# Key projections alternated on the array's row halves, and the sums over tokens with the values stationary

## The chip, the cores and the metric

The kernel runs on one core of one Trainium2 chip. A core has five engines that run side by side, each with its own queue in program order: TensorE (PE, matrix products; its weight loads are shown as PEld), VectorE (DVE), ScalarE (ACT), GpSimd (POOL) and SyncE (SP, which here issues the DMAs). TensorE reads from SBUF and writes into eight PSUM banks of 512 f32 columns on 128 partitions; GpSimd works on SBUF alone. The metric is the time of one execution on the device in microseconds.

## The reference

There are three stages: attention with a feature map (4 batches, 8 heads, 576 tokens, head size 64, 128 features, so 2 x 128 after the two exponentials), a dense layer pair with `h - tanh(h)` (512 to 2048 to 512), and a weighted mixture of four experts. The change lies in the key side of the first stage:

```python
def phi(x):
    proj = np.einsum('bhsd,df->bhsf', x, w_phi)
    proj = proj - np.max(np.abs(proj), axis=-1, keepdims=True)
    return np.concatenate([np.exp(proj), np.exp(-proj)], axis=-1)
q_p, k_p = (phi(q), phi(k))
kv = np.einsum('bhsf,bhsd->bhfd', k_p, v)      # 256 x 64 per head
z = np.sum(k_p, axis=2)                         # 256 per head
num = np.einsum('bhsf,bhfd->bhsd', q_p, kv)
den = np.einsum('bhsf,bhf->bhs', q_p, z)[..., None] + 1e-06
```

## The kernel before

The 2304 tokens are worked on in eight blocks of 288. Each block first goes through attention and then through the first half of the dense layers (eight of sixteen chunks of 128 hidden features); a second pass does the other eight chunks, and the experts come last. Attention is cut into tasks for two heads at a time: a key task (`k_task`, 16 of them) turns 576 tokens of keys and values of two heads into the sums `kv` and `z`, and a query task (`q_task`, 32 of them) uses them for 288 tokens. The key and query tasks of later blocks are laid between the dense work of earlier ones.

The order of the work is not written out by hand. Every step is a node with an engine, an estimated duration, a due time, the nodes it waits for, and the buffers and PSUM banks that it takes (`add`, `Ring`, `Bank`). `Issue.run` goes through time with these estimates and gives each engine, when it is free, the ready node that is due first; a node that wants a PSUM bank is passed over while none is free. What comes out is a fixed order of instructions on each engine, and on the chip each engine keeps to it. Four of the eight PSUM banks are handed out in this way, the other four accumulate the dense layer's output.

A key task before the change: the keys are loaded with one token of each group of four per column block and transposed (L406, L409) so that head 0 lies on partitions 0 to 63 and head 1 on 64 to 127. `proj` (L417) is called once for each head: four products of 64 x 128 stationary keys with `w_phi` moving (L422), then on VectorE the largest magnitude of each row (L429) and the subtraction (L430), and on ScalarE the two exponentials (L431, L432). The 64 remaining tokens of both heads go through L443 and L447 to L450. Then `mmk` (L455) sums over tokens, in four groups, one for each head and sign: the features are stationary (128 tokens by 128 features) and `vones` moves, which is a block of values beside a block of ones, so that columns 0 to 63 of the result are `kv` and the next ones `z`. Each group has four products (L458) and one for the remaining tokens (L459). ScalarE copies the four results out of one bank (L462) into `kv`, 128 columns for each group, of which the query task reads the first 66 (L532). All these products are in plain f32, and the profile shows each of them as two passes over the array, each with its own weight load; the dense layers use f32r, which is one pass.

On the query side, `proj` (L490) runs products for both heads in turn, head 0 on rows 0 to 63 and head 1 on rows 64 to 127, into two banks. `xf` (L542) and most of the `gl` subtractions (L236) run on GpSimd, and so does the second half of each weight split (L309). VectorE turns the first eight chunks of weights from 64-bit into 32-bit numbers (L300 to L303) during the first blocks.

Of the kernel before, what the change touches and what calls it, by code (L numbers as in the profile page):

```python
# [9 lines left out]
F32 = mybir.dt.float32  # L10
# [61 lines left out]
class Issue:  # L72
# [106 lines left out]
def attention_moe_moe_kernel(  # L179
# [45 lines left out]
    def ring(pool, n, shape, dt, name):  # L225
        return Ring([pool.tile(shape, dt, name=f"{name}{i}") for i in range(n)])
# [11 lines left out]
    def at(bk):  # L238
        return banks[bk.index]
# [12 lines left out]
    wph = const.tile([128, 128], F32R, name="wph")  # L252
    wpl = const.tile([128, 128], F32R, name="wpl")
    b_m = const.tile([128, 1], F32, name="b_m")
    pr = const.tile([128, NTT, E], F32, name="pr")
    prs = const.tile([128, NTT], F32, name="prs")
    vtiles = [att.tile([128, 14 * 64], F32, name=f"vbuf{i}") for i in range(2)]
# [4 lines left out]
    DVE.memset(b_m, THETA2)  # L262
    for vb in vtiles:
        DVE.memset(vb[:, 0:64], 1.0)
        DVE.memset(vb[:, 576:640], 1.0)
        DVE.memset(vb[:, 640:896], 0.0)
        DVE.memset(vb[0:64, 704:768], 1.0)
        DVE.memset(vb[64:128, 832:896], 1.0)
# [90 lines left out]
    kd_r = ring(att, 1, [128, 4, 128], F32, "kd")  # L359
# [3 lines left out]
    kpr_r = ring(att, 1, [128, 2, 128], F32, "kpr")  # L363
    kv_r = ring(att, 6, [128, 2, 2, 128], F32, "kv")
# [17 lines left out]
    kv_of, xt_of = {}, {}  # L382
    n_att = [0, 0]

    def vones(vb, i):
        return vb.rearrange("p (n d) -> p n d", d=64)[:, i:10:9 - i, :]

    def k_task(b, p, t0):
        rb, rrb, vb = kraw.take(), krawr.take(), v_ring.take()
        h = 2 * p  # L390
# [3 lines left out]
        ], due=t0 - 8, bufs=[rb, rrb])  # L394
        vv = vb.t
        ldv = dma([
            (vv[:, 64:576].rearrange("p (h x) -> p h x", h=2), v[b, h:h + 2, 0:512, :].rearrange("h (p r) d -> p h (r d)", r=4)),
            (vv[0:64, 640:704], v[b, h, 512:S, :]),
            (vv[64:128, 768:832], v[b, h + 1, 512:S, :]),
        ], due=t0 - 4, bufs=[vb])  # L400
        kT, km = kT_r.take(), km_r.take()
        ba, bb = Bank(), Bank()
# [11 lines left out]
        a2 = add("DVE", c_dve(64), lambda: DVE.tensor_copy(out=kT.t[:, 512:S], in_=at(bb)[:, 0:64]), [a], t0 + 0.6, [kT], frees=[bb])  # L414
        kps, es = [], []

        def proj(e, due):  # L417
            bk, kd, kp = Bank(), kd_r.take(), kp_r.take()

            def mm():  # L420
                for j in range(4):
                    PE.matmul(  # L422
                        at(bk)[:, j * 128:(j + 1) * 128], lhsT=kT.t[64 * e:64 * e + 64, j * 128:(j + 1) * 128],
                        rhs=wphi[64 * e:64 * e + 64, :], start=True, stop=True,
                    )

            m = km.t[:, 4 * e:4 * e + 4]
            a = add("PE", 0.82, mm, [a1], due, [kT, kd], bank=bk)
            a = add("DVE", c_dve(512), lambda: DVE.tensor_reduce(out=m, in_=at(bk).rearrange("p (j f) -> p j f", f=128), axis=AX.X, op=ALU.max, apply_absolute_value=True), [a], due + 1, [km], frees=[bk])  # L429
            a = add("DVE", c_dve(512), lambda: DVE.tensor_tensor(out=kd.t, in0=at(bk).rearrange("p (j f) -> p j f", f=128), in1=m.unsqueeze(2).to_broadcast([128, 4, 128]), op=ALU.subtract), [a], due + 1, [km, kd], frees=[bk])  # L430
            x1 = add("ACT", c_act(512), lambda: ACT.activation(out=kp.t[:, :, 0, :], in_=kd.t, func=ACTF.Exp), [a], due + 2, [kd, kp])  # L431
            x2 = add("ACT", c_act(512), lambda: ACT.activation(out=kp.t[:, :, 1, :], in_=kd.t, func=ACTF.Exp, scale=-1.0), [a], due + 2, [kd, kp])  # L432
# [15 lines left out]
        a = add("DVE", c_dve(128), lambda: DVE.tensor_scalar(out=kdr.t, in0=at(bk)[:, 0:128], scalar1=km.t[:, 8:9], scalar2=None, op0=ALU.subtract), [a], due + 1, [km, kdr], frees=[bk])  # L448
        r1 = add("ACT", c_act(128), lambda: ACT.activation(out=kpr.t[:, 0, :], in_=kdr.t, func=ACTF.Exp), [a], due + 2, [kdr, kpr])
        r2 = add("ACT", c_act(128), lambda: ACT.activation(out=kpr.t[:, 1, :], in_=kdr.t, func=ACTF.Exp, scale=-1.0), [a], due + 2, [kdr, kpr])  # L450
        bk2, kv = Bank(), kv_r.take()
        last = None
        for e in range(2):
            for ab in range(2):
                def mmk(e=e, ab=ab):  # L455
                    o = at(bk2)[:, (2 * e + ab) * 128:(2 * e + ab + 1) * 128]
                    for j in range(4):
                        PE.matmul(o, lhsT=kps[e].t[:, j, ab, :], rhs=vones(vv, 1 + 4 * e + j), start=j == 0, stop=False)  # L458
                    PE.matmul(o, lhsT=kpr.t[:, ab, :], rhs=vv[:, 640 + 128 * e:768 + 128 * e], start=False, stop=True)  # L459

                last = add("PE", 1.03, mmk, [es[e][ab], (r1, r2)[ab], ldv, last], t0 + 5 + e, [kps[e], kpr, vb, kv], bank=bk2)
        a = add("ACT", c_act(512, True), lambda: ACT.activation(out=kv.t.rearrange("p a b f -> p (a b f)"), in_=at(bk2), func=ACTF.Copy), [last], t0 + 8, [kv], frees=[bk2])  # L462
        kv_of[b, p] = (kv, a)

    def q_task(b, s, p, t0):
        j = 2 * b + s
# [58 lines left out]
        def side(ab):  # L525
            return at(nb[ab])[0:QP, 0:6 * DV].rearrange("p (e r d) -> p e r d", e=2, r=3)

        def mm():
            for ab, x in enumerate((ea, eb)):
                for e in range(2):  # L530
                    for r in range(3):
                        PE.matmul(side(ab)[:, e, r], lhsT=x.t[:, e, r * QP:(r + 1) * QP], rhs=kv.t[:, e, ab, 0:DV], start=True, stop=True)  # L532

        u, dn, xf = u_r.take(), dn_r.take(), xf_r.take()
        a = add("PE", 2.05, mm, [*xe, s2, kvdone], t0 + 5, [ea, eb, kv, u], banks=nb)
# [292 lines left out]
```

## Time and profile before

| what | time |
|---|---|
| median of three runs | 1500.53 us (1497.84 to 1501.63) |
| the profiled execution, as timed | 1499.14 us |
| its span in the profile | 1497.1 us |
| TensorE busy | 1481.9 us, 99% of the span |
| VectorE busy | 704.5 us, 47% |
| ScalarE busy | 521.6 us, 35% |
| GpSimd busy | 277.9 us, 19% |

The page's span is the time from the first to the last instruction of the profiled execution; some 2 us lie around it. A busy share is a mean over the whole kernel, so it hides that the attention stage loads VectorE far more than the later stages do: of the 704.5 us of VectorE, 328 lie in the first 435 us. Products overlap on TensorE, so the duration of one of them is longer than its distance to the next start; prices are read from the distances between starts.

### The profile page before, as it was taken

Reading aid. Unit: us, or ns where it says so; the run is one execution under the profiler, and the core shown is the slowest. Engines: PE = TensorE matmul, PEld = TensorE weight load, DVE = VectorE, ACT = ScalarE, POOL = GpSimd, SP = SyncE. Lnnn points to the kernel's source line nnn. Section 1 sums busy time; section 2 is a strip of 40 time slices with the busy share of each in tenths; the row PEclk is TensorE's granted clock in tenths of the full one; section 3 lists DMA queues with packets and bytes.
Section 4 is the critical chain, followed back from the end, with each engine's and each line's share of the span. In section 5 each row is a group of like instructions: output and inputs, shape, how many; then the busy total and the mean of one; then the engine's idle time right before and its main releaser. Section 6 shows DMA issues by size and latency. Waiting matters only on the chain.

```text
span 1497.1 us, 22821 instructions
## 1 busy us (share of the span) xinstructions
PE 1481.9 (99%) x9120; PEld 1313.8 (88%) x9120; DVE 704.5 (47%) x1440; ACT 521.6 (35%) x1250; POOL 277.9 (19%) x278
## 2 busy tenths in 40 slices
PE   8999999999999999999999999999999999999998
PEld 7889999999999999999888888888888888888887
DVE  6899976656676766665222122222221322222212
ACT  5565654555555655554111111111111111111101
POOL 1233111101013643436010101010101010101000
PEclk8899999999999999999999999999999999999999
DMA  6445642211113421212010000000000000000001
GB/s 173 132 153 184 202 133 64 76 37 57 60 43 109 158 81 64 67 46 80 22 29 15 29 14 29 14 22 22 28 15 28 15 29 15 22 21 7 28 29 70
DMA packets 93753, 90.70 MB, mean 61 GB/s; under 512 B 46160, under 2 KB 74960, under 8 KB 93648
## 3 DMA queue, kind: packets, MB, share of 16 engines
q1 hardware_dynamic: 93488, 89.19, 19.1%
q8 instruction: 72, 1.18, 0.3%
q14 instruction: 33, 0.27, 0.1%
q10 hardware_dynamic: 160, 0.07, 0.0%
HBM read 66.16 MB, written 23.07 MB: 60 GB/s over the span
## 4 chain that ended last, share of the span: by engine, by line
PE 93%; DVE 5%; ACT 1%; issue 0%; DMA 0%; POOL 0%; ACTq 0%; DVEq 0%
PE bank L351 40%; PE acc L351 39%; PE bank L532 4%; PE bank L458 3%; PE bank L422 2%; PE bank L516 1%; PE bank L490 1%; PE bank L459 1%; DVE wtmp L302 1%; DVE hs L585 1%; PE bank L547 0%; PE bank L476 0%; PE bank L406 0%; DVE th L587 0%; DVE wtmp L303 0%
## 5 line engine op out<-in xcount | busy, mean ns | idle before, releaser
L351 PE MATMUL bank<-x2h,wslot 128*128 128x512 f32 (+1 forms) x1280 | 392.0, 371 | 0.0
L776 DVE SCALAR_TENSOR_TENSOR hl<-bank,hh 128x512 fp32r<-128x512 f32 (+1 forms) x160 | 102.2, 639 | 595.5 <-ACT hh L775 595.5
L351 PE MATMUL acc<-wslot,hh 128*128 128x512 f32 x1152 | 356.8, 391 | 0.0
L775 ACT ACTIVATE hh<-bank 128x512 fp32r<-128x512 f32 (+1 forms) x160 | 88.8, 555 | 673.8 <-PE bank L351 673.8
L351 PEld LDWEIGHTS bank<-x2h,wslot 128*128 128x128 f32 x1280 | 233.2, 188 | 47.5
L351 PEld LDWEIGHTS acc<-wslot,hh 128*128 128x128 f32 x1152 | 213.8, 188 | 46.2
L351 PE MATMUL acc<-gh,wslot 128*128 128x288 f32 x1024 | 240.6, 303 | 0.0
L351 PE MATMUL bank<-x2l,wslot 128*128 128x512 f32 (+1 forms) x640 | 237.7, 371 | 0.0
L351 PE MATMUL acc<-wslot,hl 128*128 128x512 f32 x576 | 224.1, 389 | 0.0
L757 POOL TENSOR_TENSOR wslot<-raw,wslot 128x512 fp32r<-128x512 f32 x56 | 71.3, 1297 | 601.4 <-ACT wslot L756 581.8
L351 PEld LDWEIGHTS acc<-gh,wslot 128*128 128x128 f32 x1024 | 173.9, 188 | 3.9 <-issue 3.7
L236 POOL TENSOR_TENSOR gl<-th,gh 128x288 fp32r<-128x288 f32 x112 | 96.8, 865 | 339.2 <-ACT gh L588 225.7
L351 PE MATMUL acc<-gl,wslot 128*128 128x288 f32 x512 | 150.8, 295 | 0.0
L351 PEld LDWEIGHTS bank<-x2l,wslot 128*128 128x128 f32 x640 | 119.9, 187 | 24.0
L351 PEld LDWEIGHTS acc<-wslot,hl 128*128 128x128 f32 x576 | 108.2, 188 | 23.2
L351 PE MATMUL bank<-xt0h,wslot 128*128 128x288 f32 x512 | 115.9, 301 | 2.8 <-ACT wslot L308 1.5
L351 PE MATMUL bank<-xt1h,wslot 128*128 128x288 f32 x512 | 114.4, 298 | 0.0
L587 DVE COPY_PREDICATED th<-sq,hs 128x288 f32<-128x288 int32 x128 | 82.5, 645 | 63.4 <-ACT sq L586 63.3
L351 PEld LDWEIGHTS acc<-gl,wslot 128*128 128x128 f32 x512 | 96.5, 189 | 0.0
L586 ACT ACTIVATE sq<-sq,b_m 128x288 f32<-128x288 f32 x128 | 68.6, 536 | 62.8 <-DVE hs L585 61.8
L351 PEld LDWEIGHTS bank<-xt0h,wslot 128*128 128x128 f32 x512 | 86.4, 190 | 4.6 <-POOL wslot L309 1.8
L794 DVE SCALAR_TENSOR_TENSOR acc<-acc,pr,acc 128x512 f32<-128x512 f32 x126 | 85.9, 743 | 1.2 <-PE acc L351 1.2
(104 smaller groups left out, 1969.6 us busy)
## 6 DMA issues: line engine op xcount, KB each, us to landing
raw<-in_moe_w_dram SPq DMA_DIRECT2D x64, 256.0 KB, 2.9
raw<-in_moe_w_in_dram SPq DMA_DIRECT2D x16, 512.0 KB, 4.0
raw<-in_moe_w_out_dram SPq DMA_DIRECT2D x16, 512.0 KB, 4.4
qraw<-in_q_dram SPq DMA_DIRECT2D x32, 144.0 KB, 2.8
x2s<-x2p SPq DMA_DIRECT2D x8, 576.0 KB, 2.8
x2p<-x2s SPq DMA_DIRECT2D x8, 576.0 KB, 3.8
out_dram<-acc SPq DMA_DIRECT2D x18, 256.0 KB, 2.1
kraw<-in_k_dram SPq DMA_DIRECT2D x16, 256.0 KB, 3.5
```

The costliest lines, as they stand in the source:

```text
L236: return add("POOL", c_pool(n), lambda: POOL.tensor_tensor(out=o, in0=a, in1=b, op=op), deps, due, bufs)
L302: a = add("DVE", c_dve(DM), lambda: DVE.scalar_tensor_tensor(out=t, in0=hi, scalar=0xC0000000, in1=t, op0=ALU.bitwise_and, op1=ALU.bitwise ...
L351: PE.matmul(ps, lhsT=a, rhs=b, start=start and n == 1, stop=stop and n == 3 * len(pairs))
L422: PE.matmul(at(bk)[:, j * 128:(j + 1) * 128], lhsT=kT.t[64 * e:64 * e + 64, j * 128:(j + 1) * 128], rhs=wphi[64 * e:64 * e + 64, :], start ...
L458: PE.matmul(o, lhsT=kps[e].t[:, j, ab, :], rhs=vones(vv, 1 + 4 * e + j), start=j == 0, stop=False)
L532: PE.matmul(side(ab)[:, e, r], lhsT=x.t[:, e, r * QP:(r + 1) * QP], rhs=kv.t[:, e, ab, 0:DV], start=True, stop=True)
L586: x3 = add("ACT", c_act(N, ptr=True), lambda: ACT.activation(out=sq.t, in_=sq.t, func=ACTF.Relu, scale=-1.0, bias=b_m[:, 0:1]), [y3], due ...
L587: y4 = add("DVE", c_dve(N), lambda: DVE.copy_predicated(out=th.t, mask=sq.t.bitcast(I32), data=hs.t), [x3, y2, y3], due + 1.4, [th, sq, hs])
L757: POOL.tensor_tensor(out=wl, in0=src, in1=f32(wh), op=ALU.subtract)
L775: ACT.activation(out=hh[:, 0:n], in_=ps[:, 0:n], func=ACTF.Relu)
L776: DVE.scalar_tensor_tensor(out=hl[:, 0:n], in0=ps[:, 0:n], scalar=0.0, in1=f32(hh[:, 0:n]), op0=ALU.max, op1=ALU.subtract)
L794: DVE.scalar_tensor_tensor(out=acc[:, tt, :], in0=y, scalar=pe, in1=acc[:, tt, :], op0=ALU.mult, op1=ALU.add)
```

## The change

In a key task the two projections become one step: the eight products of both heads alternate, head 0 on rows 0 to 63 of the array and head 1 on rows 64 to 127, into two PSUM banks (the buffer `kd` is doubled for that). In the sums over tokens the roles of the operands are exchanged: a block of values (128 tokens by 64 columns) is stationary and all 256 features of a token block move, so that the result is the transpose of `kv`, head 0 on partitions 0 to 63 and head 1 on 64 to 127 of one bank. The products of the two heads alternate. The sum `z` is made apart: GpSimd adds the four token blocks of each head and the remaining tokens (`pairs`, a second addition, `rest`), and a product with a stationary block of ones sums that over the partitions (`mmz`). ScalarE copies the bank out (`kvT`), TensorE transposes it back in four pieces (`back`), and ScalarE copies `kv` and the column of `z` into a buffer of 66 columns for each group. The blocks of ones between the values go away, and the value buffers shrink.

```diff
-        def proj(e, due):
-            bk, kd, kp = Bank(), kd_r.take(), kp_r.take()
-
-            def mm():
-                for j in range(4):
-                    PE.matmul(
-                        at(bk)[:, j * 128:(j + 1) * 128], lhsT=kT.t[64 * e:64 * e + 64, j * 128:(j + 1) * 128],
-                        rhs=wphi[64 * e:64 * e + 64, :], start=True, stop=True,
-                    )
-
+        pb = [Bank(), Bank()]
+        kds = [kd_r.take(), kd_r.take()]
+
+        def proj():
+            for j in range(4):
+                for e in range(2):
+                    h0 = 64 * e
+                    PE.matmul(at(pb[e])[:, j * 128:(j + 1) * 128], lhsT=kT.t[h0:h0 + 64, j * 128:(j + 1) * 128], rhs=wphi[h0:h0 + 64, :], start=True, stop=True)
+
+        pd = add("PE", 1.05, proj, [a1], t0 + 1.2, [kT, *kds], banks=pb)
...
-        bk2, kv = Bank(), kv_r.take()
-        last = None
+        kss, zs = [], []
         for e in range(2):
-            for ab in range(2):
-                def mmk(e=e, ab=ab):
-                    o = at(bk2)[:, (2 * e + ab) * 128:(2 * e + ab + 1) * 128]
-                    for j in range(4):
-                        PE.matmul(o, lhsT=kps[e].t[:, j, ab, :], rhs=vones(vv, 1 + 4 * e + j), start=j == 0, stop=False)
-                    PE.matmul(o, lhsT=kpr.t[:, ab, :], rhs=vv[:, 640 + 128 * e:768 + 128 * e], start=False, stop=True)
-
-                last = add("PE", 1.03, mmk, [es[e][ab], (r1, r2)[ab], ldv, last], t0 + 5 + e, [kps[e], kpr, vb, kv], bank=bk2)
-        a = add("ACT", c_act(512, True), lambda: ACT.activation(out=kv.t.rearrange("p a b f -> p (a b f)"), in_=at(bk2), func=ACTF.Copy), [last], t0 + 8, [kv], frees=[bk2])
-        kv_of[b, p] = (kv, a)
+            kp, tz, ks = kps[e], tz_r.take(), ks_r.take()
+            h0 = 64 * e
+
+            def pairs(kp=kp, tz=tz):
+                POOL.tensor_tensor(out=tz.t.rearrange("p j f -> p (j f)"), in0=kp.t[:, 0:2].rearrange("p j a f -> p (j a f)"), in1=kp.t[:, 2:4].rearrange("p j a f -> p (j a f)"), op=ALU.add)
+
+            def rest(ks=ks, h0=h0):
+                POOL.tensor_tensor(out=ks.t[h0:h0 + 64], in0=ks.t[h0:h0 + 64], in1=kpr.t[h0:h0 + 64].rearrange("p a f -> p (a f)"), op=ALU.add)
+
+            a = add("POOL", c_pool(512), pairs, es[e], t0 + 4 + e, [kp, tz])
+            a = add("POOL", c_pool(256), lambda tz=tz, ks=ks: POOL.tensor_tensor(out=ks.t, in0=tz.t[:, 0], in1=tz.t[:, 1], op=ALU.add), [a], t0 + 5 + e, [tz, ks])
+            zs.append(add("POOL", c_pool(256), rest, [a, r1, r2], t0 + 5 + e, [ks, kpr]))
+            kss.append(ks)
+        bk2, bk3, kvT, kv = Bank(), Bank(), kvT_r.take(), kv_r.take()
+
+        def mmk():
+            for j in range(5):
+                for e in range(2):
+                    w = vv[:, 512 + 64 * e:576 + 64 * e] if j == 4 else vv[:, 256 * e + 64 * j:256 * e + 64 * j + 64]
+                    x = kpr.t if j == 4 else kps[e].t[:, j]
+                    PE.matmul(at(bk2)[64 * e:64 * e + 64, 0:256], lhsT=w, rhs=x.rearrange("p a f -> p (a f)"), start=j == 0, stop=j == 4)
+
+        def mmz():
+            for e in range(2):
+                PE.matmul(at(bk2)[64 * e:64 * e + 64, 256:512], lhsT=ones, rhs=kss[e].t, start=True, stop=True)
+
+        def back():
+            for i in range(4):
+                PE.transpose(out=at(bk3)[:, i * 128:(i + 1) * 128], in_=kvT.t[:, i * 128:(i + 1) * 128], identity=ident)
...
+        a = add("PE", 2.3, mmk, [*es[0], *es[1], r1, r2, ldv], t0 + 5, [*kps, kpr, vb, kvT], bank=bk2)
+        a = add("PE", 0.46, mmz, [a, *zs], t0 + 7, kss, bank=bk2)
+        a = add("ACT", c_act(512, True), lambda: ACT.activation(out=kvT.t, in_=at(bk2), func=ACTF.Copy), [a], t0 + 8, [kvT], frees=[bk2])
+        a = add("PE", 0.44, back, [a], t0 + 9, [kvT, kv], bank=bk3)
+        a1 = add("ACT", c_act(256, True), lambda: ACT.activation(out=kv_out(0, 64), in_=kv_in(0, 64), func=ACTF.Copy), [a], t0 + 9.5, [kv], frees=[bk3])
+        a2 = add("ACT", 0.1, lambda: ACT.activation(out=kv_out(64, 2), in_=kv_in(1, 2), func=ACTF.Copy), [a], t0 + 9.5, [kv], frees=[bk3])
+        kv_of[b, p] = (kv, [a1, a2])
```

## Rows read from the trace of the kernel before

**Rows 1.** Windows by block: engine busy us (instructions), granted clock, DMA share, GB/s.
```profile
161.40:219.00 57.60, 57.60 (x491) 54.64 (x490) 50.58 (x120) 34.81 (x93) 10.56 (x12) 1.00 0.56 178
219.00:277.10 58.10, 58.10 (x492) 54.96 (x492) 35.58 (x86) 31.09 (x85) 9.65 (x12) 1.00 0.21 62
...
393.30:435.00 41.70, 41.70 (x364) 40.28 (x365) 29.87 (x76) 23.08 (x69) 7.29 (x9) 1.00 0.14 51
```

**Rows 2.** Windows before 161.4 us; order PE, PEld, DVE, ACT, POOL.
```profile
20.00:100.00 80.00, 75.01 (x621) 68.71 (x620) 73.09 (x156) 50.04 (x120) 23.89 (x21) 0.94 0.48 142
100.00:161.40 61.40, 60.55 (x513) 56.71 (x513) 58.09 (x133) 37.83 (x100) 17.34 (x16) 1.00 0.56 170
```

**Rows 3.** Chain of waits from 0 to 161.4 us, shares by line.
```profile
by line: PE bank L458 12.6%; PE bank L532 10.1%; PE bank L351 9.4%; PE bank L422 9.4%; PE acc L351 6.7%; DVE wtmp L302 6.2%; issue 3.6%; PE bank L516 3.1%; DVE wtmp L303 2.9%; PE bank L459 2.9%; DVE km L429 2.3%; DVE wtmp L300 2.3%; DVE kd 
```

**Rows 4.** TensorE in order of time: start us, us, instruction, count.
```profile
101.35 0.40 PE L490 MATMUL bank<-qh,wph 64*128 64x288 f32 x2
101.59 0.30 PE L490 MATMUL bank<-ql,wph 64*128 64x288 f32 x2
101.73 0.30 PE L490 MATMUL bank<-qh,wpl 64*128 64x288 f32 x2
101.95 0.40 PE L351 MATMUL bank<-xt0h,wslot 128*128 128x288 f32 x1
102.19 0.29 PE L351 MATMUL bank<-xt0l,wslot 128*128 128x288 f32 x1
```

**Rows 5.** TensorE in order of time, 241.7 to 246.1 us.
```profile
241.75 0.29 PE L351 MATMUL acc<-gl,wslot 128*128 128x288 f32 x1
241.89 0.29 PE L351 MATMUL acc<-gh,wslot 128*128 128x288 f32 x1
242.11 1.16 PE L422 MATMUL bank<-wphi,kT 64*128 64x128 f32 x8
243.20 1.16 PE L458 MATMUL bank<-vbuf,kp 128*128 128x128 f32 x8
...
244.82 1.05 PE L458 MATMUL bank<-vbuf,kp 128*128 128x128 f32 x8
...
246.06 0.30 PE L351 MATMUL acc<-gl,wslot 128*128 128x288 f32 x1
```

**Rows 6.** Pass durations: L422 min/median/max ns; a group's busy us, mean ns; chain of waits.
```profile
L422 PE MATMUL bank<-wphi,kT x256: 272/272/579, 7.0 to 381.0; 64*128 64x128 f32 x128
...
L351 PE MATMUL bank<-x2h,wslot 128*128 128x256 f32 x256 | 50.4, 281 | 0.0
...
850.59 2.74 PE acc L351 x12
```

**Rows 7.** TensorE in order of time around L443.
```profile
119.43 0.44 PE L443 MATMUL bank<-wphi,kT 64*64 64x128 f32 x4
119.80 0.40 PE L351 MATMUL bank<-xt0h,wslot 128*128 128x288 f32 x1
```

**Rows 8.** Groups on GpSimd: busy us, mean ns, idle before (L236 from 277 to 335).
```profile
L757 POOL TENSOR_TENSOR wslot<-raw,wslot 128x512 fp32r<-128x512 f32 x56 | 71.3, 1297 | 601.4 <-ACT wslot L756 581.8 <-issue 19.6
...
L236 POOL TENSOR_TENSOR gl<-th,gh 128x288 fp32r<-128x288 f32 x7 | 5.6, 799 | 46.7 <-ACT gh L588 19.8 <-issue 16.1 <-PE acc L351 6.2
```

**Rows 9.** L302 beside GpSimd: order of time; min/median/max ns; busy us by window.
```profile
51.13 1.26 POOL L309 TENSOR_TENSOR wslot<-wtmp,wslot 128x512 fp32r<-128x512 f32 x1 [7.68 <-ACT wslot L308]
...
51.61 1.33 DVE L302 SCALAR_TENSOR_TENSOR wtmp<-raw,wtmp 128x512 uint32<-128x512 uint32 x1
...
L302 DVE SCALAR_TENSOR_TENSOR wtmp<-raw,wtmp x32: 675/691/1504, 21.8 to 205.3; 128x512 uint32<-128x512 uint32 x32
...
20.00:161.40 141.40, 20.45 (x24) 0.96 0.51 154
```

**Rows 10.** A copy of key-value sums on ScalarE and their first product on TensorE.
```profile
308.04 0.60 ACT L462 ACTIVATE kv<-bank 128x512 f32<-128x512 f32 x1
...
310.49 1.16 PE L532 MATMUL bank<-kv,ea 128*96 128x66 f32 x12
```

More of the change, by code (lines that the diff above doesn't have):

```diff
@@ L254, in attention_moe_moe_kernel @@
     b_m = const.tile([128, 1], F32, name="b_m")
+    ones = const.tile([128, 64], F32, name="ones")
     pr = const.tile([128, NTT, E], F32, name="pr")
     prs = const.tile([128, NTT], F32, name="prs")
-    vtiles = [att.tile([128, 14 * 64], F32, name=f"vbuf{i}") for i in range(2)]
+    vtiles = [att.tile([128, 10 * 64], F32, name=f"vbuf{i}") for i in range(2)]
     make_identity(nc, ident)
@@ L262, in attention_moe_moe_kernel @@
     DVE.memset(b_m, THETA2)
+    DVE.memset(ones, 1.0)
     for vb in vtiles:
[L264 to L268, printed above, removed]
+        DVE.memset(vb[64:128, 512:576], 0.0)
+        DVE.memset(vb[0:64, 576:640], 0.0)
     ACT.dma_start(out=wphi[0:64, :], in_=w_phi)
@@ L358, in attention_moe_moe_kernel @@
     kT_r = ring(att, 1, [128, S], F32, "kT")
-    kd_r = ring(att, 1, [128, 4, 128], F32, "kd")
+    kd_r = ring(att, 2, [128, 4, 128], F32, "kd")
     kdr_r = ring(att, 1, [128, 128], F32, "kdr")
@@ L362, in attention_moe_moe_kernel @@
     kp_r = ring(att, 2, [128, 4, 2, 128], F32, "kp")
-    kpr_r = ring(att, 1, [128, 2, 128], F32, "kpr")
-    kv_r = ring(att, 6, [128, 2, 2, 128], F32, "kv")
+    kpr_r = ring(att, 2, [128, 2, 128], F32, "kpr")
+    kvT_r = ring(att, 1, [128, 512], F32, "kvT")
+    kv_r = ring(att, 6, [128, 2, 2, DV], F32, "kv")
+    tz_r = ring(att, 1, [128, 2, 256], F32, "tz")
+    ks_r = ring(att, 2, [128, 256], F32, "ks")
     qh_r = ring(att, 2, [128, N], F32R, "qh")
@@ L396, in k_task @@
         ldv = dma([
-            (vv[:, 64:576].rearrange("p (h x) -> p h x", h=2), v[b, h:h + 2, 0:512, :].rearrange("h (p r) d -> p h (r d)", r=4)),
-            (vv[0:64, 640:704], v[b, h, 512:S, :]),
-            (vv[64:128, 768:832], v[b, h + 1, 512:S, :]),
+            (vv[:, 0:512].rearrange("p (h x) -> p h x", h=2), v[b, h:h + 2, 0:512, :].rearrange("h (p r) d -> p h (r d)", r=4)),
+            (vv[0:64, 512:576], v[b, h, 512:S, :]),
+            (vv[64:128, 576:640], v[b, h + 1, 512:S, :]),
         ], due=t0 - 4, bufs=[vb])
@@ L415, in k_task @@
         kps, es = [], []
-        def proj(e, due):
-            bk, kd, kp = Bank(), kd_r.take(), kp_r.take()
-            def mm():
-                for j in range(4):
-                    PE.matmul(
-                        at(bk)[:, j * 128:(j + 1) * 128], lhsT=kT.t[64 * e:64 * e + 64, j * 128:(j + 1) * 128],
-                        rhs=wphi[64 * e:64 * e + 64, :], start=True, stop=True,
-                    )
-            m = km.t[:, 4 * e:4 * e + 4]
[L428 to L432, printed above, removed]
@@ new lines, in k_task @@
+        pb = [Bank(), Bank()]
[7 more added lines that the diff above has]
+        for e in range(2):
+            bk, kd, kp, due = pb[e], kds[e], kp_r.take(), t0 + 2 + e
+            m = km.t[:, 4 * e:4 * e + 4]
+            a = add("DVE", c_dve(512), lambda bk=bk, m=m: DVE.tensor_reduce(out=m, in_=at(bk).rearrange("p (j f) -> p j f", f=128), axis=AX.X, op=ALU.max, apply_absolute_value=True), [pd], due, [km], frees=[bk])
+            a = add("DVE", c_dve(512), lambda bk=bk, m=m, kd=kd: DVE.tensor_tensor(out=kd.t, in0=at(bk).rearrange("p (j f) -> p j f", f=128), in1=m.unsqueeze(2).to_broadcast([128, 4, 128]), op=ALU.subtract), [a], due, [km, kd], frees=[bk])
+            x1 = add("ACT", c_act(512), lambda kd=kd, kp=kp: ACT.activation(out=kp.t[:, :, 0, :], in_=kd.t, func=ACTF.Exp), [a], due + 1, [kd, kp])
+            x2 = add("ACT", c_act(512), lambda kd=kd, kp=kp: ACT.activation(out=kp.t[:, :, 1, :], in_=kd.t, func=ACTF.Exp, scale=-1.0), [a], due + 1, [kd, kp])
@@ new lines, in mmz, with kv_out, kv_in @@
+        def mmz():
+            for e in range(2):
+                PE.matmul(at(bk2)[64 * e:64 * e + 64, 256:512], lhsT=ones, rhs=kss[e].t, start=True, stop=True)
+        def back():
+            for i in range(4):
+                PE.transpose(out=at(bk3)[:, i * 128:(i + 1) * 128], in_=kvT.t[:, i * 128:(i + 1) * 128], identity=ident)
+        def kv_out(lo, n):
+            return kv.t[:, :, :, lo:lo + n].rearrange("p e a d -> p a e d")
+        def kv_in(i, n):
+            return at(bk3)[:, 256 * i:256 * i + 256].rearrange("p (a e d) -> p a e d", a=2, e=2)[:, :, :, 0:n]
@@ L531, in mm @@
                     for r in range(3):
-                        PE.matmul(side(ab)[:, e, r], lhsT=x.t[:, e, r * QP:(r + 1) * QP], rhs=kv.t[:, e, ab, 0:DV], start=True, stop=True)
+                        PE.matmul(side(ab)[:, e, r], lhsT=x.t[:, e, r * QP:(r + 1) * QP], rhs=kv.t[:, e, ab], start=True, stop=True)
         u, dn, xf = u_r.take(), dn_r.take(), xf_r.take()
-        a = add("PE", 2.05, mm, [*xe, s2, kvdone], t0 + 5, [ea, eb, kv, u], banks=nb)
+        a = add("PE", 2.05, mm, [*xe, s2, *kvdone], t0 + 5, [ea, eb, kv, u], banks=nb)
         due = t0 + 7
```

4 lines of the change are left out of this document (removed).

## The prediction

> **What bounds the kernel now.** I read the page first: the time is one TensorE story, 1481.9 of 1497.1 us busy, so the question is in which stretches TensorE really sets the pace. The windows by block answer that [rows 1]. One block of 288 tokens ends with the evacuation of its four accumulators, and the reader is to see that the three blocks between 219 and 393.3 us last 58.1 us each with VectorE busy for some 36 (the first stands for the three), while the next block, which is the first without key work, lasts 41.7. Each of the three holds two key tasks, so a key task costs (58.1 - 41.7) / 2 = 8.2 us of wall time there: in that stretch TensorE is the bound, and what a key task saves on TensorE is saved in full. The block from 161.4 to 219 has two key tasks too, but VectorE is busy 50.58 of 57.6, so it can give back 7 us at most. Before 161.4 us lie the other eight key tasks, and there VectorE is busy 73.09 + 58.09 = 131.2 of the 141.4 us after 20 us [rows 2]; the chain of waits runs through both engines, with 24.9% of it on key matmuls (L422, L458, L459) and at least 13% on VectorE's [rows 3]. No instruction that the change touches lies behind 393.3 us.
>
> **Prices.** A switch of the array's shape costs time at both ends. Ordinary 288-column passes start 0.14 us apart (241.75 to 241.89); the first row-half pass starts 0.22 after the last of them, and the eight passes of L422 take 1.09 until the next start [rows 5]. A full-array group of 10 passes takes 1.11 (244.82 to 246.06 less one 0.13 spacing), so 8 passes at 0.111 are 0.89. The excursion therefore costs 0.09 before, 0.20 inside, and 0.10 behind (the first pass after one takes 0.24 instead of 0.13: 101.95 to 102.19 [rows 4]): 0.39 us together. For halves of 64 stationary columns the first load is half as long, so I count 0.34.
>
> **Projections.** Before, two tasks of eight passes, each its own excursion: 2 x (0.89 + 0.39) = 2.56 us. After, one task of sixteen passes in eight pairs. The query projection already alternates like this: six 288-column passes on row halves take 0.60 us (101.35 to 101.95), where six in turn would take 0.80 [rows 4]; and the four 128-column passes of L443 on opposite quadrants take 0.37 with their switch [rows 7], where four in turn are 0.44 without one. So a pair costs one pass, and the new task 0.89 + 0.39 = 1.28: 1.28 us saved. In turn it would be 1.78 + 0.39 = 2.17, 0.39 saved; I take 1.28, since L490 is the same split.
>
> **Sums over tokens.** Before: 4 groups of 10 passes, 4 x 1.11 = 4.44 us. After: 10 products, two passes each, of 64 stationary by 256 moving columns; then 2 products with ones (4 passes) in a task of their own, as they wait for GpSimd; then 4 transposes. No row shows a two-pass f32 product with 256 moving columns. A 128-column pass of that type lasts 272 ns, almost what a 256-column pass of the one-pass type lasts (281) [rows 6], so a column seems to take two ticks. From below: the one-pass price, 0.13 for 288 columns. From above: a 512-column pass, twelve in 2.74 us, 0.228 each [rows 6]. I take 0.228, as the 272 against 281 puts it there. If the two column halves run together, the products cost 10 x 0.228 + 0.34 = 2.62, the ones 2 x 0.228 + 0.34 = 0.80, the transposes 4 x 0.111 = 0.44: 3.86 us, 0.58 less than 4.44. Without overlap it is 20 x 0.228 + 0.34 = 4.90, 4 x 0.228 + 0.34 = 1.25 and 0.44: 6.59 us, 2.15 more. No row shows two column halves under the same 128 rows; the nearest are the row halves and the quadrants, both of which overlap, so I take 3.86.
>
> The Trainium skill's "TensorE: Matmul & The Clock Gate" (Part 3, The mechanism) says that a weight load overlaps matmuls in flight only if it goes to another row group; column halves have the same row group, and by that rule the sum would be that of the serial case or above. The trace here speaks against the rule: L458 reloads all 128 rows before each pass, and its passes still follow each other at 0.111 us.
>
> **One task** thus gives 1.28 + 0.58 = 1.86 us of TensorE.
>
> **What is added elsewhere.** GpSimd gets six additions per key task: two of 512 and four of 256 columns. A 512-column subtraction takes 1.30 and a 288-column one 0.80 [rows 8], so 2 x (1.30 + 0.75 + 0.75) = 5.6 us, 90 us in sixteen tasks, on an engine busy 9.65 of 58.1 in the PE-bound blocks [rows 1]. It fits there. But it isn't free for VectorE: L302, which reads two SBUF tensors, took 1.33 us where a GpSimd subtraction had started 0.5 us before it and ended at 52.39, against a median of 0.69 [rows 9]. Operations of that sort (L302, L303, L585, L587, L300) hold by my estimate a quarter of VectorE's time before 161.4 us (L302 alone 20.45 us, in 24 pieces [rows 9]), arriving about every 2 us; an addition of 0.75 to 1.3 us meets one in about half the cases and holds it for some 0.4 us, so 48 additions cost about 10 us there. The bounds are 0 and 48 x 0.64 = 31. VectorE's idle time there is 10.2 us. ScalarE gets two small copies of 256 and 8 columns beside the one of 512 (0.60 [rows 10]), at most 1.2 us per task; it is busy 31.09 of 58.1 [rows 1], so nothing. The memsets shrink by a us at the start, under the first loads. DMA issues stay three per value load: nothing.
>
> The new path to the key-value sums is longer: after the last exponential come the products, GpSimd's additions, the ones, a copy, the transposes and two copies, some 4 us more. A product that reads the sums starts 1.85 us after they were written (308.64 to 310.49 [rows 10]), so in every second block two query tasks move back by some 2 us. TensorE has other work in its order there; I cost it at nothing, and at up to 1 us per task if the order leaves no cover.
>
> **The sum.** Three PE-bound blocks: 6 x 1.86 = 11.2 us. The block from 161.4: 3.7 us saved on TensorE, and VectorE's slack of 7 less some 3 allows it; I take 3.3. The eight tasks before: 15 us saved on TensorE, but VectorE's slack there (10.2) is about eaten by the shared access; I take 2, with -9 to +12 as ends. Together 16.5 us. The profiled execution took 1499.14 us (span 1497.1 and 2.0 around it), so 1482.6; it lies 1.4 us below the median of the runs, 1500.53, and I give 1483.
>
> **Rivals.**
> 1. *The column halves run in turn* (slower). Per task 2.15 - 1.28 = 0.87 us more; eight tasks after 161.4 us give 7, those before some 5 with VectorE's waits: 1512. For it: no row has this split. Against it: every split that the trace shows overlaps. The point from which it decides: with p for a pair, the new task costs 1.28 + 12p + 1.12, the old one 2.56 + 4.44, so p = 0.38 instead of 0.228 eats the gain.
> 2. *VectorE gives the start back.* The GpSimd additions hold VectorE for some 20 us before 161.4 us, the lower end above (-9), and the next block gains nothing: 11.2 - 9 = 2, so 1498. For it: VectorE is 91 to 95% busy there. Against it: the waits fall on the operations without PSUM input alone.
> 3. *TensorE waits for the ones' operand.* The additions stand in GpSimd's order behind subtractions that wait for a block's ScalarE results; half a us of standing TensorE in each task, and TensorE held in order behind it, gives 8 us back: 1491. Against it: in the PE-bound blocks TensorE does not stand once now.
> 4. *A moving column takes one tick*, as for the other type: products 10 x 0.13 + 0.34 = 1.64, ones 0.60, transposes 0.44: 1.76 + 1.28 = 3.04 us per task; 18 for the three blocks, 4 and 3 before them: 25, so 1474.
>
> **Chances.** Forecast 0.60 (1476 to 1490 on its own), the first rival 0.13, the second 0.12, the third 0.10, the fourth 0.05. A difference under 0.3%, 4.5 us, can't be told from none. The forecast, the third and the fourth are faster; the second is shared between faster (0.04) and the same (0.08); the first is slower, and 0.01 stands for worse forms of the second and third. So 0.78, 0.08 and 0.14. The range 1470 to 1501 leaves out most of the first rival and the deep end of the fourth.
>
> **What would show it.** Right: the PE-bound blocks shrink from 58.1 to about 54.4 us; the sixteen projection passes of a task take about 1.1 us; the twenty passes of products about 2.3 to 2.5, with two starting at once; GpSimd's new lines about 5.6 us per task; L302, L585 and L587 longer in the mean. Wrong: products over 4 us per task (first rival); the first evacuation later than 161.4 us (second); idle time on TensorE before the ones' product, ended by GpSimd (third). A block of 58 us or more would refute the forecast.

## The result, and the profile after

The changed kernel takes 1506.95 us (median of five, 1506.72 to 1507.82) against 1500.53 of the kernel before in the same session: a ratio of 1.0051, 95% interval 1.0034 to 1.0068. It is half a per cent slower; the forecast was 1483, with a range from 1470 to 1501, and the result lies outside it. The profiled execution has a span of 1506.0 us.

TensorE's work shrank, from 1481.9 to 1458.8 us busy. That is 23 us, where sixteen tasks at the forecast's 1.86 us give 30, and TensorE now stands idle. The windows by block (engine busy us in the order PE, PEld, DVE, ACT, POOL, then clock and DMA) show where:

```profile
20.00:100.00 80.00, 62.38 (x451) 45.94 (x452) 72.06 (x127) 43.14 (x111) 43.69 (x40) 0.83 0.47 135
100.00:166.30 66.30, 58.76 (x486) 50.47 (x486) 63.66 (x126) 38.35 (x103) 33.50 (x30) 0.97 0.40 121
166.30:231.10 64.80, 60.17 (x505) 51.63 (x503) 63.51 (x130) 39.98 (x106) 31.36 (x31) 0.97 0.53 168
231.10:287.70 56.60, 55.16 (x473) 48.64 (x473) 45.14 (x101) 32.54 (x92) 23.28 (x25) 1.00 0.35 108
287.70:342.30 54.60, 53.61 (x464) 47.18 (x462) 37.55 (x88) 31.29 (x89) 20.46 (x24) 1.00 0.22 66
342.30:397.60 55.30, 54.31 (x467) 47.77 (x467) 39.45 (x91) 31.81 (x90) 18.49 (x21) 1.00 0.13 44
397.60:443.80 46.20, 46.20 (x406) 44.31 (x407) 32.85 (x83) 25.75 (x76) 8.37 (x10) 1.00 0.13 46
```

Beside [rows 1, 2]: the first evacuation comes at 166.3 instead of 161.4 us, the second at 231.1 instead of 219.0. TensorE is busy 62.38 of 80 us between 20 and 100 us, where it was 75.01, and the granted clock there is 0.83 of full speed instead of 0.94, so some of those us ran at the lower of its two levels (1.2 and 2.4 GHz). Over the whole execution the mean granted clock is 0.988 against 0.992. As a mix of the two levels that is some 36 us at the lower one against 24, so up to 6 of the 8.9 us between the spans can be the clock's. Why it was granted less these runs do not show.

Behind the second evacuation the blocks take 56.6, 54.6 and 55.3 us instead of 58.1 each (the last of these evacuations is at 397.6). The forecast's figure, 54.4 us for a block where TensorE is the bound, is met in the second of them. TensorE is not quite the bound any more: it stands 1.4, 1.0 and 1.0 us in the three blocks, and they give 7.8 us where 11.2 were forecast. The block behind them takes 46.2 instead of 41.7, since the key tasks have slid back: the last key-value sums are copied at 401 us, inside it, where before they were done at 388. The sum of the differences: +12.1 - 1.5 - 3.5 - 2.8 + 4.5 = 8.8 us, which is the difference of the spans, 8.9.

TensorE in order of time in the block from 287.7 (start us, us, instruction, count) shows that the array does what the change says:

```profile
309.81 1.16 PE L424 MATMUL bank<-wphi,kT 64*128 64x128 f32 x16
310.90 0.44 PE L442 MATMUL bank<-wphi,kT 64*64 64x128 f32 x4
...
316.71 1.95 PE L474 MATMUL bank<-kp,vbuf 128*64 128x256 f32 x16
318.49 0.60 PE L474 MATMUL bank<-kpr,vbuf 128*64 128x256 f32 x4
319.02 0.86 PE L549 MATMUL bank<-ident,pq 128*96 128x128 f32 x6
...
322.87 0.70 PE L478 MATMUL bank<-ks,ones 128*64 128x256 f32 x4
323.50 1.23 PE L565 MATMUL bank<-kv,ea 128*96 128x66 f32 x12
```

Sixteen projection passes take the 1.09 us that eight took [rows 5]. The twenty passes of products take 2.31 us (316.71 to 319.02), and the first sixteen of them 1.78, so a pair of column halves costs 0.2225 us. The duration of one pass (ns: least, median, most) tells how that comes about:

```profile
L474 PE MATMUL bank<-kp,vbuf x256: 379/379/689, 14.2 to 392.5; 128*64 128x256 f32 x128
```

It lasts 379 ns, where a 256-column pass of f32r lasts 281 [rows 6], and in the trace the two passes of a pair start 7 ns apart: two halves at once, at two ticks per moving column. The ones take 0.63 us until the next start.

What went wrong is on VectorE. Its groups of SBUF operations (busy us, mean ns of one) in the kernel before:

```profile
L302 DVE SCALAR_TENSOR_TENSOR wtmp<-raw,wtmp 128x512 uint32<-128x512 uint32 x32 | 26.8, 837 | 0.3
L303 DVE SCALAR_TENSOR_TENSOR wtmp<-raw,wtmp 128x512 uint32<-128x512 uint32 x32 | 23.3, 727 | 0.2
L301 DVE TENSOR_SCALAR wtmp<-wtmp 128x512 uint32<-128x512 uint32 x32 | 14.0, 439 | 0.5
L585 DVE SCALAR_TENSOR_TENSOR hs<-sq,hs 128x288 f32<-128x288 f32 x128 | 67.6, 528 | 0.0
```

and in the changed kernel, where the same lines are L301, L302, L300 and L618, with one that reads PSUM (L616) and the three additions on GpSimd:

```profile
L618 DVE SCALAR_TENSOR_TENSOR hs<-sq,hs 128x288 f32<-128x288 f32 x128 | 76.5, 598 | 0.0
L616 DVE SCALAR_TENSOR_TENSOR hs<-bank,sq 128x288 f32<-128x288 f32 x128 | 57.8, 452 | 54.1 <-ACT th L615 52.4
L301 DVE SCALAR_TENSOR_TENSOR wtmp<-raw,wtmp 128x512 uint32<-128x512 uint32 x32 | 36.5, 1140 | 0.5
L302 DVE SCALAR_TENSOR_TENSOR wtmp<-raw,wtmp 128x512 uint32<-128x512 uint32 x32 | 30.5, 954 | 0.1
L300 DVE TENSOR_SCALAR wtmp<-wtmp 128x512 uint32<-128x512 uint32 x32 | 20.8, 652 | 0.2
...
L458 POOL TENSOR_TENSOR tz<-kp 128x512 f32<-128x512 f32 x32 | 44.2, 1382 | 55.4 <-ACT kp L433 45.6 <-PE bank L509 9.7
L461 POOL TENSOR_TENSOR ks<-ks,kpr 64x256 f32<-64x256 f32 x32 | 27.3, 853 | 3.7 <-ACT kpr L449 1.6
L464 POOL TENSOR_TENSOR ks<-tz 128x256 f32<-128x256 f32 x32 | 26.6, 831 | 1.9
```

The weight conversion got longer by 9.7, 7.2 and 6.8 us in these three lines; the operation on PSUM kept its 452 ns. The additions take 98 us, 6.1 per key task. How a hold looks is seen around 114 us, in VectorE's, GpSimd's and TensorE's rows of the changed kernel:

```profile
111.98 1.11 DVE L301 SCALAR_TENSOR_TENSOR wtmp<-raw,wtmp 128x512 uint32<-128x512 uint32 x1
...
113.38 0.44 DVE L596 TENSOR_TENSOR xt1l<-bank,xt1h 128x288 fp32r<-128x288 f32 x1
113.74 4.40 DVE L302 SCALAR_TENSOR_TENSOR wtmp<-raw,wtmp 128x512 uint32<-128x512 uint32 x1
118.06 0.45 DVE L616 SCALAR_TENSOR_TENSOR hs<-bank,sq 128x288 f32<-128x288 f32 x1
...
111.74 0.79 POOL L464 TENSOR_TENSOR ks<-tz 128x256 f32<-128x256 f32 x1
112.50 1.24 POOL L236 TENSOR_TENSOR gl<-th,gh 128x288 fp32r<-128x288 f32 x1
113.70 0.73 POOL L461 TENSOR_TENSOR ks<-ks,kpr 64x256 f32<-64x256 f32 x1
114.40 1.29 POOL L458 TENSOR_TENSOR tz<-kp 128x512 f32<-128x512 f32 x1
115.66 1.25 POOL L308 TENSOR_TENSOR wslot<-wtmp,wslot 128x512 fp32r<-128x512 f32 x1
116.88 0.71 POOL L464 TENSOR_TENSOR ks<-tz 128x256 f32<-128x256 f32 x1
...
114.57 0.29 PE L350 MATMUL acc<-gh,wslot 128*128 128x288 f32 x1
118.93 0.47 PE L405 MATMUL bank<-ident,kraw 128*128 128x128 f32 x1 [4.07 <-DVE th L617]
```

L302, a 0.68 us operation, took 4.40 us, through four GpSimd instructions (three additions and a weight split) that follow each other without a gap; it ended only behind the last. TensorE then stood 4.07 us for an operation behind it in VectorE's queue. Not every operation is held through a chain: L301 at 111.98 us took 1.11 us and was done while the next GpSimd instruction, the subtraction at 112.50, still ran. Of eight of these conversions (L301, L302) that were held by a GpSimd instruction with another close behind it, six stayed held through the next, and two did not. The Trainium skill's "GPSIMD Engine Reference" (Specifications) says that GpSimd's SBUF interfaces are shared with VectorE, in contention with its operations that have two SBUF inputs or run in a two-port mode. The rows agree for L301, L302 and L618, which have two SBUF inputs and got longer, and for L616, which has one in PSUM and did not. L300 has one SBUF input and got longer too; whether it runs in a two-port mode no row shows. L620, a predicated copy with two SBUF inputs, hardly changed (645 to 657 ns).

The chain of waits up to the first evacuation now has 13.8% on L301 and L302, which in the kernel before, as L302 and L303, had 9.1% [rows 3]:

```profile
by line: issue 11.2%; DVE wtmp L302 8.2%; DVE wtmp L301 5.6%; PE bank L474 4.8%; DVE km L430 4.1%; PE bank L565 3.8%; PE bank L350 3.8%; DVE wtmp L299 3.7%; DMA raw<-in_moe_w_out_dram 3.7%; DVE wtmp L300 3.5%; PE bank L549 3.4%; DVE kd L431
```

Between 20 and 231.1 us TensorE's waits are ended by VectorE and ScalarE, but for one gap of 3.7 us in which the profile shows no wait; none is put down to GpSimd.

### The profile page after: what moved, and what is told of

The parts are those of the page before. It is cut to its first block, busy times and chain, and to the rows that moved or that the text cites. A ratio compares the mean times of both kernels' runs of the same rounds, so it can differ in the third digit from the quotient of the medians.

```text
span 1506.0 us, 22610 instructions
## 1 busy us (share of the span) xinstructions
PE 1458.8 (97%) x8928; PEld 1258.8 (84%) x8928; DVE 741.0 (49%) x1435; ACT 527.0 (35%) x1282; POOL 378.5 (25%) x374
## 4 chain that ended last, share of the span: by engine, by line
PE 84%; DVE 11%; ACT 2%; issue 2%; DMA 1%; SPq 0%; POOL 0%; ACTq 0%; DVEq 0%
PE bank L350 38%; PE acc L350 37%; PE bank L565 3%; DVE hs L618 2%; PE bank L549 1%; DVE wtmp L302 1%; DVE wtmp L301 1%; PE bank L474 1%; DVE km L430 1%; DVE th L620 1%; DVE kd L431 1%; PE bank L523 1%; DVE hs L616 1%; DVE th L617 1%; DVE wtmp L299 1%
## 5 line engine op out<-in xcount | busy, mean ns | idle before, releaser
L350 PEld LDWEIGHTS acc<-wslot,hh 128*128 128x128 f32 x1152 | 213.8, 188 | 46.2
L236 POOL TENSOR_TENSOR gl<-th,gh 128x288 fp32r<-128x288 f32 x112 | 98.2, 877 | 229.9 <-ACT gh L621 198.4
L620 DVE COPY_PREDICATED th<-sq,hs 128x288 f32<-128x288 int32 x128 | 84.1, 657 | 58.2 <-ACT sq L619 58.2
L350 PEld LDWEIGHTS bank<-xt1h,wslot 128*128 128x128 f32 x512 | 86.0, 189 | 0.8 <-DVE wtmp L299 0.4
```

Of the source, the lines that this page charges most:

```text
L236: return add("POOL", c_pool(n), lambda: POOL.tensor_tensor(out=o, in0=a, in1=b, op=op), deps, due, bufs)
L350: PE.matmul(ps, lhsT=a, rhs=b, start=start and n == 1, stop=stop and n == 3 * len(pairs))
L620: y4 = add("DVE", c_dve(N), lambda: DVE.copy_predicated(out=th.t, mask=sq.t.bitcast(I32), data=hs.t), [x3, y2, y3], due + 1.4, [th, sq, hs])
```

## The experiments

All times are medians; the kernel before, run beside them, took 1497.8 to 1499.3 us, and 1500.5 beside the changed kernel. A difference between runs of different sessions is good to 2 or 3 us.

**The changed kernel without the additions** (e1).

```diff
-            a = add("POOL", c_pool(512), pairs, es[e], t0 + 4 + e, [kp, tz])
...
-                PE.matmul(..., lhsT=ones, rhs=kss[e].t, start=True, stop=True)
+                PE.matmul(..., lhsT=ones, rhs=kc, start=True, stop=True)
```

> The changed kernel without GpSimd's 96 additions; the product with ones reads a constant tile, so the denominators are not the reference's. Theory P (the additions hold VectorE's operations that read SBUF, above all the weight conversion, and the stretch before the second evacuation is VectorE's): VectorE's busy time falls back to about 705 us, the second evacuation comes before 219 us instead of at 231, and the time is 1470 to 1486 us. Theory W (the longer path from the exponentials to the key-value sums, or the banks that it holds, keeps TensorE waiting): only the wait for GpSimd goes, and the time stays at 1495 us or more. Theory O (the order that the list scheduler makes from the new estimates is worse): 1503 us or more.

Measured: 1478.30 us, ratio 0.9848 (0.9831 to 0.9864). VectorE busy 708.8 us; second evacuation at 210.8. Theory P holds, W and O in these forms fall: all else that the change did is worth 21 us of gain, and the additions, with the order that was planned with them, cost 28.7 us.

**The additions made, but waited for by nobody** (e2).

```diff
-        a = add("PE", 0.46, mmz, [a, *zs], t0 + 7, kss, bank=bk2)
+        a = add("PE", 0.46, mmz, [a], t0 + 7, [], bank=bk2)     # reads kc
```

> The changed kernel with all 96 additions on GpSimd, but the product with ones reads a constant tile, so nobody on TensorE waits for them (the denominators are not the reference's). Theory P: the additions still hold VectorE, VectorE busy 735 us or more, time 1498 to 1508 us. Theory W in the form that TensorE's wait for the additions costs the time: 1475 to 1490 us, as without the additions.

Measured: 1500.23 us, ratio 0.9999 (0.9986 to 1.0012), VectorE busy 735.0. The presence of the additions is worth 21.9 us. The other 6.7 are not shown to be the wait of the ones' product: without it the list scheduler makes another order of all work, and in the changed kernel 0.3 us of TensorE's idle time before this product is put down to GpSimd.

**The kernel before with the additions, unused** (e3).

```diff
+            z = add("POOL", c_pool(512), pairs, es[e], t0 + 4 + e, [tz])
+            z = add("POOL", c_pool(256), lambda tz=tz, ks=ks: POOL.tensor_tensor(out=ks.t, ...), [z], t0 + 5 + e, [tz, ks])
+            add("POOL", c_pool(256), rest, [z, r1, r2], t0 + 5 + e, [ks])
```

> The kernel before, with the same six additions per key task issued on GpSimd after the exponentials, on a constant tile, their results unused. TensorE's work is that of before. Theory P: the additions alone lengthen the start; VectorE busy 730 us or more, second evacuation at 230 us or later, time 1512 to 1530 us. Theories W and O: nobody waits for the results, 1498 to 1504 us.

Measured: 1514.94 us, ratio 1.0091 (1.0075 to 1.0106): 15.7 us more. VectorE's 724.0 us fell short of the 730 expected. The windows show that all of it is paid up to the second evacuation; the third is a block where TensorE is the bound, and it takes the 58.10 of [rows 1] with twice GpSimd's work:

```profile
20.00:175.60 155.60, 141.57 (x1131) 130.64 (x1130) 147.52 (x291) 88.14 (x219) 84.60 (x78) 0.92 0.49 146
175.60:234.80 59.20, 58.16 (x490) 54.56 (x489) 51.59 (x116) 34.34 (x93) 22.95 (x24) 1.00 0.51 159
292.90:351.00 58.10, 58.10 (x492) 54.96 (x491) 36.34 (x87) 31.10 (x86) 19.73 (x23) 1.00 0.21 62
```

The first evacuation comes 14.2 us later than before. In the window up to it TensorE stands 14.0 us, where it stood 5.8 [rows 2]; and a granted clock of 0.92 over 155.6 us, against 0.96 over 141.4 [rows 9], costs up to 12.4 us instead of 5.7. So a good half of what the additions cost here comes as TensorE's idle time, and up to 7 us as a lower clock, for which no run shows the reason.

**The alternating projections alone** (e4: `proj` and the two `kd` buffers of the change in the kernel before).

> The kernel before with the projections of the two heads alternating on the row halves, the sums over tokens as before. Theory P: no additions, so 1.28 us per key task are saved where TensorE is the bound (eight tasks, 10 us) and some at the start: 1483 to 1491 us. Theory W in the form that the projection's two banks at once starve TensorE at the start: 1497 us or more.

Measured: 1483.98 us, ratio 0.9887 (0.9872 to 0.9902). A block with two key tasks:

```profile
268.20:323.70 55.50, 55.50 (x492) 52.86 (x491) 35.55 (x87) 30.82 (x85) 8.86 (x11) 1.00 0.22 65
```

It takes 55.5 instead of 58.1 us, 1.3 per task where 1.28 was forecast.

**New sums in the last six key tasks alone** (e5).

```diff
+        if b * NP + p < NEWFROM:      # 10: the sums of before
...
+            return
```

> Projections alternate in all sixteen key tasks; the new sums with GpSimd's additions are used in the last six key tasks alone, those that lie in the blocks where TensorE is the bound, and the sums of before in the first ten. Theory P: the additions cost nothing behind the second evacuation, and the sums give about 0.5 us per task there: 1479 to 1483 us, 1 to 5 us below the kernel with the projections alone (1484.0). If the additions cost the same wherever they are (23 us for sixteen tasks beside the kernel without them), six of them cost 8 us: 1486 us or more.

Measured: 1482.05 us, ratio 0.989 (0.9869 to 0.9911). The gain over e4 is within the intervals. The additions still cost something in those blocks, as a look ahead to e11 shows, where VectorE makes them and a block takes 53.8 us; here TensorE stands 0.9 us in it:

```profile
316.20:371.40 55.20, 54.27 (x467) 47.78 (x466) 39.20 (x91) 31.83 (x89) 18.33 (x21) 1.00 0.13 44
```

**The additions on VectorE** (e6: `DVE` for `POOL` in the six additions, planned with VectorE's estimates).

> The changed kernel with the six additions per key task on VectorE instead of GpSimd; at 0.6, 0.33 and 0.33 us (scaled from VectorE's other operations of 512 columns) they add 2.5 us per task, 40 us in all, to VectorE. If VectorE's time at the start is what counts, and GpSimd's additions cost it 2.0 us per task, this is as slow or slower: 1503 to 1515 us. If it is GpSimd's queue (the subtractions and attention rows that stand behind the additions) that costs the time, 1484 to 1494 us.

Measured: 1483.33 us, ratio 0.99 (0.9879 to 0.992). VectorE was busy 745.2 us, more than in the changed kernel (741.0), and yet the kernel is 23.6 us faster. So VectorE's busy time by itself does not set the time, as I had held. It pointed to GpSimd's queue; the next pair speaks against that.

**Without the weight conversion, without and with the additions** (e7, e8).

```diff
-        a = add("DVE", c_dve(DM, True), lambda: DVE.tensor_scalar(... scalar1=TINY ...
-        a = add("DVE", c_dve(DM, True), lambda: DVE.tensor_scalar(... scalar1=5, scalar2=2 ...
-        a = add("DVE", c_dve(DM), lambda: DVE.scalar_tensor_tensor(... 0xC0000000 ...
-        a = add("DVE", c_dve(DM), lambda: DVE.scalar_tensor_tensor(... scalar=29 ...
```

> The kernel before without the four VectorE operations that turn the dense layer's weights from 64-bit into 32-bit numbers (the weights are then wrong); the base for the next kernel. VectorE loses 80 us, 50 of them before the second evacuation, so TensorE becomes the bound there: 1465 to 1485 us by theory P.

> The same without the weight conversion, with the unused additions of the earlier experiment on GpSimd. Theory P (the additions cost time because VectorE is the bound at the start and is held by them): with VectorE relieved they cost 0 to 4 us beside the kernel without the conversion and the additions, where they cost 15.6 us before. Theory Q (the additions delay what stands behind them in GpSimd's queue, and that delays TensorE): 10 to 16 us again.

Measured: 1486.21 and 1489.58 us, ratios 0.9917 (0.9896 to 0.9939) and 0.9941 (0.9919 to 0.9964). The base missed its window by a us. With VectorE relieved the additions cost 3.4 us instead of 15.7, though they stand in GpSimd's queue as before. The mean granted clock, 0.994 against 0.998, can make up those 3.4 us by itself. That speaks against GpSimd's queue and for VectorE's load; it is not proof, since a kernel with slack on VectorE could hide a late GpSimd too.

**Order and engine apart** (e9 to e13). The estimates given to the list scheduler also make the order of all other work, so e6 differs from the changed kernel in two things. e9 has e6's order with the additions issued on GpSimd, e10 the changed kernel's order with them on VectorE; TensorE's and ScalarE's instructions are the same within a row of the table below. e12 and e13 issue no additions in either order.

```diff
-            a = add("POOL", c_pool(512), pairs, es[e], t0 + 4 + e, [kp, tz])
+            a = add("DVE", c_dve(512), pairs, es[e], t0 + 4 + e, [kp, tz])      # e9: pairs stays on POOL
...
+            a = add("POOL", c_pool(512), lambda: None, es[e], t0 + 4 + e, [kp, tz])   # e12
```

> The order of the kernel with the additions on VectorE (1483.3 us), instruction for instruction on TensorE, ScalarE and the DMA queue, but with the additions issued on GpSimd at the places where that order has them. Theory H (the additions on GpSimd hold VectorE wherever they stand): VectorE busy 725 us or more, 1497 to 1510 us, like the changed kernel. Theory O (the list scheduler's order with the additions planned on GpSimd is the bad part): 1478 to 1487 us.

> The order of the changed kernel (1507 us), with the additions issued on VectorE at the places where that order has them on GpSimd. Theory H: VectorE does 1.6 us of additions per head in its own queue and is not held; 1480 to 1490 us, like the kernel that planned them there. Theory O: 1500 us or more.

> The order of the changed kernel, made with the additions planned on GpSimd, but the additions are not issued and the product with ones reads a constant tile (denominators not the reference's). Nothing is held and nothing waited for; only the order is that of the changed kernel. If the order by itself costs time: 1487 to 1498 us. If the order is only bad together with the additions (their holds and the wait): 1476 to 1483 us, like the kernel that never planned them (1478.3).

> The same with the order that was made with the additions planned on VectorE (1483.3 us with them issued there, 1496.6 with them issued on GpSimd); no additions are issued. If an addition on VectorE costs little there: 1475 to 1482 us, and GpSimd's additions then cost 15 to 21 us in one and the same order of all other work. If this order is bad too: over 1483 us, which would mean that the additions in VectorE's queue cost nothing.

| order planned with the additions on | issued on GpSimd | issued on VectorE | not issued |
|---|---|---|---|
| GpSimd | 1506.95 | 1501.66 (e10) | 1477.36 (e12) |
| VectorE | 1496.62 (e9) | 1483.33 (e6) | 1476.92 (e13) |

e9 lands a little below what H expected and e10 where O expected it, so neither theory holds alone. The last column settles it: without additions both orders are the same, and the same as the order that never planned any (e1, 1478.30). The order costs nothing by itself. In the changed kernel's order the additions cost 29.6 us on GpSimd and 24.3 on VectorE; in the order that was made with a cost on VectorE for them, 19.7 and 6.4. The 19.7 are not all holds: in e9 TensorE waits 8.3 us for the additions themselves before the ones (total us, times, longest):

```profile
PE bank L478 <- POOL ks L461: 8.3, 10, 2.4
```

The weight conversion in e12, with the changed kernel's order and no additions, is back to the durations of the kernel before (here L303 and L304):

```profile
L303 DVE SCALAR_TENSOR_TENSOR wtmp<-raw,wtmp 128x512 uint32<-128x512 uint32 x32 | 26.5, 827 | 0.5
L304 DVE SCALAR_TENSOR_TENSOR wtmp<-raw,wtmp 128x512 uint32<-128x512 uint32 x32 | 23.7, 739 | 0.1
```

As the changed kernel and e12 have one order, their windows compare like with like. Up to the first evacuation, the changed kernel and then e12:

```profile
0.00:166.30 166.30, 135.08 (x1046) 107.34 (x1048) 145.96 (x279) 91.22 (x235) 83.35 (x82) 0.91 0.48 136
0.00:151.00 151.00, 134.34 (x1044) 106.43 (x1046) 127.77 (x280) 91.05 (x234) 40.98 (x40) 0.91 0.53 150
```

VectorE is busy 18.2 us longer for the same work, with 42 additions on GpSimd, and the evacuation comes 15.3 us later. In the next block of e12 VectorE is busy 55.59 us, where the changed kernel has 63.51 in its window from 166.3, 7.9 us more:

```profile
151.00:208.10 57.10, 57.10 (x505) 49.78 (x504) 55.59 (x131) 39.37 (x106) 12.79 (x13) 1.00 0.61 190
```

**The best of both** (e11: e5 with its additions on VectorE).

> Projections alternate in all tasks, the new sums in the last six key tasks alone, their additions on VectorE, which has 20 us to spare in each block there. The blocks behind the second evacuation should take 53.5 us instead of 55.1 with the additions on GpSimd: 1474 to 1479 us, below the 1482.05 of the kernel with them on GpSimd. If VectorE's own additions are in the way there: 1481 us or more.

Measured: 1480.20 us, ratio 0.9879 (0.9858 to 0.99), just outside the expected window, with the blocks as expected:

```profile
315.30:369.10 53.80, 53.80 (x468) 47.79 (x467) 41.43 (x103) 31.34 (x89) 6.57 (x8) 1.00 0.13 45
```

It beats both kernels by over 1%. Its interval overlaps those of e4 and e5, so that it beats the projections alone is not shown.

## Why the prediction was wrong

*The bound by block* was right for the kernel before and for e1, where TensorE does not stand in the blocks behind the second evacuation (53.6 and 53.7 us). In the changed kernel it stands 3.4 us in three of them.

*The prices on TensorE* were right for the projections and a little too high for the rest. Projections: 1.28 us forecast, 1.3 measured alone. Products, ones and transposes: e1 against e4 runs from the second to the sixth evacuation in 203.3 instead of 208.3 us, some 0.8 us for each of the six tasks, where 0.58 was forecast. A load of 64 columns is not half as long as one of 128 (0.14 against 0.19 us), yet the ones cost 0.63 us and not 0.80. The first and the fourth rival fall with the pair of 0.2225 us: the halves overlap, and a column takes two ticks. The sentence of the Trainium skill's "TensorE: Matmul & The Clock Gate" (Part 3, The mechanism) on row groups, from which the serial case would follow, does not hold for this row either, whose halves share all 128 rows.

*The additions' cost to VectorE* is the step that failed: "an addition of 0.75 to 1.3 us meets one in about half the cases and holds it for some 0.4 us, so 48 additions cost about 10 us there", and from it "2" us of gain at the start. Beside e12, which has the same order without the additions, the cost is 18.2 us of VectorE up to the first evacuation, and 7.9 in the next block, where the prediction took some 3: 26 us instead of 13. The bound of 31 that I had named for the start was not passed. Almost all of it became time: the second evacuation comes at 231.1 us instead of e12's 208.1, and against the kernel before the stretch up to it lost 12.1 us instead of gaining 5.3.

Why the term was too small: I took each addition as a hold of its own. They come in chains, beside the weight splits and the other subtractions, and an operation that meets a chain can be held through several of its instructions: 4.40 us at 113.74. In the kernel before, the longest L303 took 1.64 us, and in e12 two conversions took over 2; in the changed kernel six did, 18.5 us together where their median would make 4.1.

I also weighed the holds against VectorE's idle time. That the hold fell on work that no estimate made room for is a reading, not a measurement: e6 puts 40 us of additions on VectorE itself and loses 5 us against e1, as the scheduler planned room for them, while e10 leaves them unplanned and loses 24. That the range ended at 1501 although the bounds of this cost allowed 21 us more than I took is the fault in its form.

*The second rival* was thus the one that came: its premise, some 20 us of holds before 161.4 us, is near the 18.2 measured. Its price of 1498 was too low, since it put nothing for the next block, which lost 7.2 us, and gave the stretch behind it the full 11.2 us, where the changed kernel gained 3.3. *The third* is not shown in the changed kernel: its sign, idle TensorE before the ones ended by GpSimd, is 0.3 us, and the 6.7 us between it and e2 hold another order as well. In e9 the sign is there, with 8.3 us.

*Moving back* of the key tasks, costed at nothing, gave 4.5 us back in the block behind the last key task. e1 shows the same (45.8 us for that block) without the additions, so it does not come from the additions; the longer path and the order are the likely reasons. Within e1's gain it is only a shift.

What stays open: why the changed kernel's order takes the additions so badly even on VectorE (24.3 us against 6.4). That it was planned without any VectorE time for them is the plain reading, and e6 bears it out; which step of the order it is was not tried. Open too is why the clock was granted less with the additions. Nor was it tried to spread the additions so that GpSimd's instructions don't follow each other.

## What to carry to other kernels

Work moved to an engine that looks idle can be paid for by another engine, as VectorE paid here for GpSimd's additions: count how long a chain of its instructions is, not how long one is, and look up what stands behind the held operation. A scheduler that works with estimates should be given such a cost: the same additions cost 24.3 us on VectorE where they were not planned there, and 6.4 where they were. And a change of two parts is worth trying by its parts: here the alternating projections alone give 1.1%, and the other part took all of it back.

## What the hardware showed that was not expected

- A VectorE operation on two SBUF tensors can go without a turn through several GpSimd instructions that follow each other: 0.68 us became 4.40 over four of them, and 3.96 in another chain. It does not always: L301 at 111.98 us got its turn between two of them.

```profile
82.61 3.96 DVE L301 SCALAR_TENSOR_TENSOR wtmp<-raw,wtmp 128x512 uint32<-128x512 uint32 x1
```

- The same 96 additions cost 19.7 us on GpSimd and 6.4 on VectorE, in one order of all other work.
- Two column halves of the array under the same 128 rows take f32 passes at once: a pair of 256 moving columns costs 0.2225 us, the price of one 512-column pass of f32r, 0.228 [rows 6].
